# A cached-attention decode block with wq loaded by rows of 112, 8 and 8, and w1 loaded and multiplied block by block

## The chip, the cores and the metric

The kernel runs on one core of one Trainium2 chip. The metric is the device time of one execution in microseconds. A profile of one execution goes with it; its span runs from the first to the last instruction of the program.

## The reference

Four rows (batch 4, one token each) of width 640 pass through an attention block with a cache of 4096 keys and values for each of 32 heads of 128, and then through a dense block with the Mish activation. All inputs are bf16.

```python
def _A_ref(x, k_cache, v_cache, wq, wo):
    q = (x @ wq).reshape(B, Sq, H, Dh).transpose(0, 2, 1, 3)
    scores = jnp.einsum("bhqd,bhkd->bhqk", q, k_cache) * (Dh ** -0.5)
    o = jnp.einsum("bhqk,bhkd->bhqd", _softmax(scores), v_cache)
    return o.transpose(0, 2, 1, 3).reshape(B, Sq, H * Dh) @ wo

def _B_ref(x, w1, b1, w2):
    h = jnp.einsum("bsd,df->bsf", x, w1) + b1
    sp = jnp.log1p(jnp.exp(-jnp.abs(h))) + jnp.where(h > 0, h, 0)
    return jnp.einsum("bsf,fd->bsd", h * jnp.tanh(sp), w2)

h = x + _A_ref(_layernorm(x), k_cache, v_cache, wq, wo)
out = h + _B_ref(_layernorm(h), w1, b1, w2)
```

Sizes: wq is 640 x 4096, wo 4096 x 640, w1 640 x 1728, w2 1728 x 640. Keys and values are 134 MB each.

## The kernel before

The program sets its own order: what is written first is issued first on each engine. Everything that is large comes by DMA on SP's queue; only x and b1 come by ACT's queue.

Three slots of 64 KB per partition hold all large data in turn. The first holds wq (with x and b1 behind it). wq is read with five consecutive rows on each of the 128 partitions, so one partition's share is 40,960 contiguous bytes. Then keys and values alternate: `load_kv` brings the keys (`kt`) or the values (`vt`) of eight heads of one batch row, 8 MB, and there are 16 such units u. A load is issued when its slot comes free. The values of the last unit come in four transfers (`VQ`), the others in one.

- `qT_ps` (L200): q for all heads, 160 products; `q_broadcast` spreads one unit's q over the partitions.
- `scores(u)`: DVE multiplies the keys by q in place (L261), PE sums over d with an identity (L268), DVE reduces (L249).
- `softmax(u)`: maximum, broadcast, and eight exponentials on ACT (L307).
- `pv(u-1)`: 64 products with the values (L323). `close(u)` normalizes the result (L338 to L352).

After the last unit's scores the slot `wend` takes wo in four transfers (L386) and w1 in two (L389). `w1_sb` has five row blocks of 128 rows each; `W1P = 4` of them come in the first transfer, the fifth in the second. The slot `wend2` takes w2: its last 64 rows (L395), and the rest in three transfers for chunks 0 to 7, 8 to 11 and 12 (L397).

Then, once per execution and everything in transposed form (width on the partitions):

- `regroup` and `project` (L419 to L436), four times, one for each part of wo: the attention output times wo into `yT`.
- L459: `hT` = x + yT. `column_means` (L463, L467) gives the mean; L474 writes `h2T` = hT minus the mean, the input of the dense block, not yet divided by the deviation.
- h1 (L489): F = 1728 is cut into 13 chunks of 128 and one of 64, fourteen in all. Each chunk is a sum over the five row blocks of w1, so there are 70 products into `h1_ps`. `h1_pass(c, dcs)` does chunk c for the row blocks `dcs`: first all fourteen chunks with the first four blocks, then all fourteen with the fifth. After the fifth chunk of the first round stands the variance (L467), whose square root and reciprocal give `rstd`.
- L514 to L540: scaling, bias and Mish on DVE and ACT.
- y2T (L549): 70 products with w2, the 64-row chunk first, then chunks 0 to 12. Then the sum with hT, a transpose (L561) and the store (L570).

Of the kernel before, what the change touches and what calls it, by code (L numbers as in the profile page):

```python
# [16 lines left out]
def kernel(  # L17
# [13 lines left out]
    nc = tc.nc  # L31
# [5 lines left out]
    DC = D // 128  # L37
# [19 lines left out]
    C2 = F // 128  # L57
    FM = C2 * 128
    FREM = F - FM
    FC = C2 + 1  # L60
    W2P = (0, 8, 12, C2)
    W1P = 4

    ctx.enter_context(tc.manual_schedule())

# [13 lines left out]
    def slot(name):  # L79
        return slots.tile([128, SLOT], BF16, tag="kv", name=name)  # L80
# [13 lines left out]
    wq_sb = first[:, 0 : DC * H * Dh].rearrange("p (c n) -> p c n", c=DC)  # L94
# [3 lines left out]
    b1_row = first[0:1, o0 + 2 * D : o0 + 2 * D + F]  # L98

    nc.scalar.dma_start(out=x_bf, in_=x_rows[:, :])  # L100
    nc.sync.dma_start(out=wq_sb, in_=A_wq.rearrange("(p c) n -> p c n", c=DC))
    nc.scalar.dma_start(out=b1_row, in_=B_b1.rearrange("(o f) -> o f", o=1))
    kts, vts = {}, {}
    kts[0] = load_kv("kt", A_k_cache, 0)
# [53 lines left out]
    for src, dst in ((ln1_v, xT), (x_v, xT_res)):  # L158
# [10 lines left out]
        out=own1[:, :], in_=ident[:, :].rearrange("p (i k) -> p i k", i=G), axis=AX.X, op=ALU.add  # L169
    )  # L170
    nc.vector.tensor_scalar(
        out=own[:, :], in0=own1[:, :], scalar1=-1.0, scalar2=1e30, op0=ALU.add, op1=ALU.mult
    )
    nc.vector.tensor_reduce(
        out=sel[:, :, :],
        in_=ident[:, :].rearrange("p (t i r) -> p r i t", t=CT, r=RQ),
# [5 lines left out]
        out=dq_f[:, :], in_=ident[:, :].rearrange("p (q j) -> p q j", j=J), axis=AX.X, op=ALU.add  # L182
# [4 lines left out]
        out=j_f[:, :], in_=ident[:, :].rearrange("p (q j) -> p j q", j=J), axis=AX.X, op=ALU.add  # L187
# [3 lines left out]
    def f_chunk(rows, c):  # L191
        if c < C2:
            return rows[:, 0:FM].rearrange("p (f k) -> p k f", k=C2)[:, c, :], 128
        return rows[:, FM:F], FREM
# [3 lines left out]
    for h in range(H):  # L198
        for c in range(DC):
            nc.tensor.matmul(  # L200
                qT_ps[:, h, :],
                lhsT=wq_sb[:, c, h * Dh : (h + 1) * Dh],
                rhs=xT[:, c, :],
                start=(c == 0),
                stop=(c == DC - 1),
# [3 lines left out]
    for c in range(FC):  # L209
        cols, fw = f_chunk(b1_row, c)  # L210
# [171 lines left out]
    w1_sb = wend[:, nwo : nwo + DC * F].rearrange("p (c f) -> p c f", c=DC)  # L382
# [2 lines left out]
    for o in range(NO):  # L385
        nc.sync.dma_start(out=wo_sb[:, o], in_=wo_view[:, o])  # L386
    w1_view = B_w1.rearrange("(c p) n -> p c n", p=128)
    for c0, c1 in ((0, W1P), (W1P, DC)):
        nc.sync.dma_start(out=w1_sb[:, c0:c1], in_=w1_view[:, c0:c1])  # L389
    wend2 = slot("wend2")  # L390
    nw2 = FC * D
    w2_sb = wend2[:, 0 : C2 * D].rearrange("p (k n) -> p k n", k=C2)
# [8 lines left out]
    def scratch(n, dt=FP32):  # L401
        a = at[0]
        w = n * (2 if dt == FP32 else 1)
        w += w % 2
        at[0] = a + w
        ap = wend2[:, a : a + w]
        return ap.bitcast(FP32)[:, 0:n] if dt == FP32 else ap[:, 0:n]
# [53 lines left out]
    def column_means(src, name):  # L461
        part = scratch(N)
        nc.vector.tensor_reduce(  # L463
            out=part, in_=src.rearrange("p c n -> p n c"), axis=AX.X, op=ALU.add
        )
        m_ps = ps.tile([128, N], FP32, tag="oT", name=f"{name}_ps")
        nc.tensor.matmul(m_ps[:, :], lhsT=mean_f, rhs=part, start=True, stop=True)  # L467
        return m_ps
# [4 lines left out]
    for dst in (h2T, hc):  # L473
        nc.vector.tensor_tensor(  # L474
            out=dst,
# [7 lines left out]
    h1_ps = ps.tile([128, FC, N], FP32, tag="qq", name="h1_ps")  # L483
    nc.vector.memset(h1_ps[FREM:128, FC - 1, :], 0.0)
    rstd = scratch(N)
    def h1_pass(c, dcs):
        fw = f_chunk(w1_sb[:, 0, :], c)[1]
        for dc in dcs:
            nc.tensor.matmul(  # L489
                h1_ps[0:fw, c, :],  # L490
                lhsT=f_chunk(w1_sb[:, dc, :], c)[0],
                rhs=h2T[:, dc, :],
                start=(c == 0 and dc == 0),
                stop=(c == C2 - 1 and dc == DC - 1),
            )

    for c in range(FC):
        h1_pass(c, range(W1P))
        if c == 4:
            v_ps = column_means(sq, "var")  # L500
            std = scratch(N)
            nc.scalar.activation(
                out=std, in_=v_ps[:, :], func=ACT.Sqrt, bias=eps_t[:, :], scale=1.0
            )
            nc.scalar.activation(out=dummy[:, :], in_=eps_t[0:N, :], func=ACT.Exp)
            nc.vector.reciprocal(out=rstd, in_=std)
    for c in (C2, *range(C2)):
        h1_pass(c, range(W1P, DC))

    def fcn():  # L510
        return scratch(FC * N).rearrange("p (c n) -> p c n", c=FC)
# [3 lines left out]
        out=h1n,  # L515
# [6 lines left out]
        out=h1s,  # L522
# [8 lines left out]
        out=tb, in0=ta, scalar=2.0, in1=ta, op0=ALU.add, op1=ALU.mult  # L531
# [3 lines left out]
        out=tc_, in0=tb, scalar1=-0.5, scalar2=-1.0, op0=ALU.mult, op1=ALU.add  # L535
# [5 lines left out]
        out=act_t, in0=td, scalar=1.0, in1=h1s, op0=ALU.add, op1=ALU.mult  # L541
# [4 lines left out]
    for i, (w2, c) in enumerate(w2_of):  # L546
        rows = 128 if c < C2 else FREM
        for dc in range(DC):
            nc.tensor.matmul(  # L549
                y2T[:, dc, :],  # L550
                lhsT=w2[:, dc * 128 : (dc + 1) * 128],
                rhs=act_t[0:rows, c, :],
                start=(i == 0 and dc == 0),
                stop=(i == FC - 1 and dc == DC - 1),
# [3 lines left out]
        out=oT.rearrange("p n c -> p c n"), in0=hT, in1=y2T[:, :, :], op=ALU.add  # L558
# [4 lines left out]
        lhsT=oT.rearrange("p n c -> p (n c)"),  # L563
        rhs=ident[:, :],
        start=True,
        stop=True,
# [35 lines left out]
```

## Time and profile before

| what | value |
|---|---|
| time, median of 3 runs | 671.0 us (670.92 to 671.01) |
| the profiled execution's own time | 670.93 us |
| its span | 669.1 us |
| moved by DMA | 283.78 MB, mean 424 GB/s |
| busy: PE, DVE, ACT | 385.3, 353.3, 86.8 us |
| granted TensorE clock, 100 to 580 us | 0.84 |
| granted TensorE clock from 640 us on | 0.50 |

The span has two stretches. Until about 650 us units of keys and values stream in, and the engines work on each when it has landed. From there on only the projection and the dense block are left. In the timeline each row has its start, its length, the engine, the line, the tiles, the number of instructions and, in brackets, how long the engine had been idle and what ended that. A q after an engine's name is its instruction queue. In the page's list of DMA issues the last number is the time from issue to landing.

### The profile page before, as it was taken

The page shows a single profiled execution, that of the slowest core. Times are in us where ns is not written, and L with a number is a line of the kernel's source. Part 1 is how long each engine was busy: PE and PEld are TensorE (multiplying, and loading weights), DVE is VectorE, ACT ScalarE, POOL GpSimd, SP SyncE. Part 2 cuts the span into 40 slices and gives each one's busy share as a digit, 9 for nine tenths or more (in the row PEclk, how much of TensorE's full clock was granted, in tenths as well). Part 3 has the DMA queues.
Part 4 walks back from the last instruction along what each step waited for, and adds up shares of the span by engine and source line. Part 5 has one row for each costly group of instructions (what it writes and reads, how often), then busy time and mean ns, then how long its engine had stood idle before and what let it go on. Part 6 is the DMA issues. An engine that isn't in the chain of part 4 may idle for free.

```text
span 669.1 us, 6430 instructions
## 1 busy us (share of the span) xinstructions
PE 385.3 (58%) x2793; PEld 182.5 (27%) x2793; DVE 353.3 (53%) x314; ACT 86.8 (13%) x314; POOL 1.4 (0%) x10
## 2 busy tenths in 40 slices
PE   0366758385572738467282855737285673728755
PEld 0322323132231313223031322313132331313345
DVE  2078848183664818275381926648192654818321
ACT  0102020202020020202002020110202020020211
POOL 0000000000000000000000000000000000000000
PEclk9998979689696968979698886969788696978955
DMA  9999999999999999999999999999999999999995
GB/s 377 440 439 432 439 432 435 432 439 424 427 432 439 440 431 416 431 440 439 428 431 428 435 432 439 435 428 435 436 431 432 427 424 435 436 428 415 427 413 187
DMA packets 7013, 283.78 MB, mean 424 GB/s; under 512 B 771, under 2 KB 967, under 8 KB 1736
## 3 DMA queue, kind: packets, MB, share of 16 engines
q1 hardware_dynamic: 6974, 283.35, 98.4%
q8 instruction: 22, 0.36, 0.2%
q14 instruction: 7, 0.06, 0.0%
q10 hardware_dynamic: 10, 0.01, 0.0%
HBM read 283.35 MB, written 0.01 MB: 423 GB/s over the span
## 4 chain that ended last, share of the span: by engine, by line
DMA 59%; DVE 25%; PE 12%; issue 2%; SPq 0%; DVEq 0%; ACT 0%
DMA kt<-in_A_k_cache_dram 55%; DVE kt L261 21%; PE s L268 6%; DMA wend<-in_B_w_dram 5%; PE o L323 4%; DVE s_sb L249 3%; PE h_ps L489 1%; DVE pm L287 1%; PE tr L289 0%; PE tr L300 0%; DVE mx L293 0%; PE y2T L549 0%; SPq L386 0%; DVE otn L352 0%; DVE rl L351 0%
## 5 line engine op out<-in xcount | busy, mean ns | idle before, releaser
L268 PE MATMUL s<-kt,ident 128*128 128x512 bf16 x1024 | 269.5, 417 | 223.4 <-DVE kt L261 223.4
L261 DVE TENSOR_TENSOR kt<-kt,qb 128x4096 bf16<-128x4096 bf16 x128 | 288.2, 2284 | 190.6 <-DMA kt<-in_A_k_cache_dram 190.6
L268 PEld LDWEIGHTS <-ident 128*128 128x128 bf16 x1024 | 108.7, 106 | 377.8 <-issue 148.2
L307 ACT ACTIVATE e<-s_sb,nb 128x256 bf16<-128x256 f32 x128 | 63.1, 494 | 218.7 <-DVE nb L302 218.7
L249 DVE TENSOR_REDUCE s_sb<-s 128x64 f32<-128x512 f32 x64 | 44.0, 688 | 54.4 <-PE s L268 32.5
L323 PE MATMUL o<-vt,e 128*32 128x512 bf16 x1024 | 66.2, 415 | 4.3 <-DMA vt<-in_A_v_cache_dram 4.3
L235 ACT CAST qb<-qb_ps 128x128 bf16<-128x128 f32 x16 | 4.3, 266 | 306.4 <-PE qb_ps L227 306.4
L323 PEld LDWEIGHTS <-e 128*32 128x32 bf16 x1024 | 28.1, 104 | 34.3 <-issue 13.7
L307 ACT ACTIVATION_READ_ACCUMULATOR e<-s_sb,nb 128x1 f32 x128 | 23.8, 186 | 0.0
L289 PE MATMUL tr<-ident_f,pm 128*1 128x128 f32 x32 | 6.1, 270 | 21.3 <-DVE pm L287 21.3
L342 PE MATMUL oT<-sel,o_sb 128*128 128x8 f32 x128 | 17.5, 263 | 1.1 <-ACT o_sb L331 1.1
L342 PEld LDWEIGHTS oT<-sel,o_sb 128*128 128x128 f32 x128 | 16.4, 200 | 1.3 <-ACT o_sb L331 1.3
L351 DVE RECIPROCAL rl<-oT 128x8 f32<-128x8 f32 x16 | 3.2, 202 | 16.9 <-PE oT L342 16.9
L331 ACT COPY o_sb<-o 128x512 f32<-128x512 f32 x16 | 9.1, 569 | 14.6 <-PE o L323 14.6
L200 PE MATMUL qT_ps<-xT,first 128*128 128x4 bf16 x160 | 4.4, 166 | 10.9 <-DMA first<-in_A_wq_dram 10.9
L289 PEld LDWEIGHTS tr<-ident_f,pm 128*1 128x1 f32 x32 | 1.8, 80 | 28.7 <-issue 28.7
L300 PE MATMUL tr<-mx,nscale 1*128 1x8 f32 x32 | 6.1, 262 | 5.9 <-DVE mx L293 5.9
L293 DVE TENSOR_REDUCE mx<-tr 1x8 f32<-1x128 f32 x16 | 4.5, 278 | 9.0 <-PE tr L289 9.0
L214 DVE COPY b1T<-b_ps 128x13 f32<-128x13 f32 x1 | 0.2, 173 | 14.7 <-PE b_ps L211 14.7
L300 PEld LDWEIGHTS tr<-mx,nscale 1*128 1x128 f32 x32 | 4.7, 182 | 10.6 <-DVE mx L293 10.6
L200 PEld LDWEIGHTS <-first 128*128 128x128 bf16 x160 | 4.3, 104 | 11.0 <-DMA first<-in_A_wq_dram 11.0
L338 PEld LDWEIGHTS oT<-rs,ones_f 128*128 128x128 f32 x32 | 6.1, 198 | 3.3 <-issue 1.3
(77 smaller groups left out, 77.0 us busy)
## 6 DMA issues: line engine op xcount, KB each, us to landing
vt<-in_A_v_cache_dram SPq DMA_DIRECT2D x4, 2048.0 KB, 44.0
first<-in_A_wq_dram SPq DMA_DIRECT2D x1, 5120.0 KB, 15.6
wend<-in_A_wo_dram SPq DMA_DIRECT2D x4, 1280.0 KB, 21.2
wend<-in_B_w_dram SPq DMA_DIRECT2D x1, 1728.0 KB
wend<-in_B_w_dram SPq DMA_DIRECT2D x1, 1280.0 KB, 21.0
wend<-in_B_w_dram SPq DMA_DIRECT2D x1, 640.0 KB, 20.2
wend<-in_B_w_dram SPq DMA_DIRECT2D x1, 432.0 KB, 28.2
kt<-in_A_k_cache_dram SPq DMA_DIRECT2D x16, 47.9
```

Source lines behind the costliest of these rows:

```text
L200: nc.tensor.matmul(qT_ps[:, h, :], lhsT=wq_sb[:, c, h * Dh : (h + 1) * Dh], rhs=xT[:, c, :], start=(c == 0), stop=(c == DC - 1),)
L249: nc.vector.tensor_reduce(out=s_sbs[u][:, part * RP : (part + 1) * RP], in_=s_ps[:, :, :], axis=AX.X, op=ALU.add,)
L261: nc.vector.tensor_tensor(out=kt[:, :, d0 : d0 + DQ], in0=kt[:, :, d0 : d0 + DQ], in1=qbs[u][:, d0 : d0 + DQ].unsqueeze(1).to_broadcast([1 ...
L268: nc.tensor.matmul(s_ps[:, :, :], lhsT=ident[:, :], rhs=kt[:, :, d : d + W], start=(d == 0), stop=(d == Dh - W),)
L287: nc.vector.tensor_reduce(out=pm[:, :], in_=s_sb[:, :], axis=AX.X, op=ALU.max)
L289: nc.tensor.matmul(tr_ps[0:1, 0:128], lhsT=pm[:, :], rhs=ident_f[:, :], start=True, stop=True)
L300: nc.tensor.matmul(nb_ps, lhsT=nscale[:, :], rhs=mx[:, :], start=True, stop=True)
L307: nc.scalar.activation(out=e2[:, :, i, :], in_=s_sb[:, :].rearrange("p (g r) -> p g r", r=RQ), func=ACT.Exp, bias=nb[:, i : i + 1], scale= ...
L323: nc.tensor.matmul(o_ps[t : t + G * RQ, :], lhsT=e2[:, g, :, :], rhs=vt[:, g * RQ : (g + 1) * RQ, :], start=(g < CT), stop=(g >= NGV - CT),)
L331: nc.scalar.copy(out=o_sb[:, :], in_=o_ps[:, :])
L342: nc.tensor.matmul(oT_ps[:, 0, :], lhsT=o_sb[:, r * Dh : (r + 1) * Dh], rhs=sel[:, r, :], start=(r == 0), stop=(r == RQ - 1),)
L489: nc.tensor.matmul(h1_ps[0:fw, c, :], lhsT=f_chunk(w1_sb[:, dc, :], c)[0], rhs=h2T[:, dc, :], start=(c == 0 and dc == 0), stop=(c == C2 - ...
```

## The change

wq comes by three transfers on SP's queue instead of one: partitions 0 to 111, 112 to 119 and 120 to 127. w1 comes by five transfers of one row block each, instead of one of four blocks and one of one. The h1 products are reordered: five rounds, one for each row block, of fourteen products (chunk 0, the 64-wide chunk, then 1 to 12). The variance stands after the second round, that is after 28 products instead of 20. The number of products stays the same. wo and w2 are loaded as before.

```diff
-    W1P = 4
...
-    nc.sync.dma_start(out=wq_sb, in_=A_wq.rearrange("(p c) n -> p c n", c=DC))
+    wq_view = A_wq.rearrange("(p c) n -> p c n", c=DC)
+    for p0, p1 in ((0, 112), (112, 120), (120, 128)):
+        nc.sync.dma_start(out=wq_sb[p0:p1], in_=wq_view[p0:p1])
...
-    for c0, c1 in ((0, W1P), (W1P, DC)):
-        nc.sync.dma_start(out=w1_sb[:, c0:c1], in_=w1_view[:, c0:c1])
+    for c in range(DC):
+        nc.sync.dma_start(out=w1_sb[:, c], in_=w1_view[:, c])
...
-    def h1_pass(c, dcs):
-        fw = f_chunk(w1_sb[:, 0, :], c)[1]
-        for dc in dcs:
+    for dc in range(DC):
+        for c in (0, C2, *range(1, C2)):
+            lhsT, fw = f_chunk(w1_sb[:, dc, :], c)
             nc.tensor.matmul(
                 h1_ps[0:fw, c, :],
-                lhsT=f_chunk(w1_sb[:, dc, :], c)[0],
+                lhsT=lhsT,
                 rhs=h2T[:, dc, :],
-                start=(c == 0 and dc == 0),
-                stop=(c == C2 - 1 and dc == DC - 1),
-            )
-
-    for c in range(FC):
-        h1_pass(c, range(W1P))
-        if c == 4:
+                start=(dc == 0 and c == 0),
+                stop=(dc == DC - 1 and c == C2 - 1),
+            )
+        if dc == 1:
             v_ps = column_means(sq, "var")
...
-    for c in (C2, *range(C2)):
-        h1_pass(c, range(W1P, DC))
```

## The prediction

> **What bounds the kernel now.** I read the page first: its slices, then its chain, then its DMA parts.
>
> ```profile
> DMA  9999999999999999999999999999999999999995
> ...
> q1 hardware_dynamic: 6974, 283.35, 98.4%
> q8 instruction: 22, 0.36, 0.2%
> ...
> q10 hardware_dynamic: 10, 0.01, 0.0%
> ...
> DMA 59%; DVE 25%; PE 12%; issue 2%; SPq 0%; DVEq 0%; ACT 0%
> ```
>
> The 16 DMA engines are full in 39 of 40 slices, and 283 MB over 669 us leave nothing to gain but what comes before the first byte and after the last. So I went to the end: the chain in order of time, then the timeline of PE and of SP's queue.
>
> ```profile
> 626.13 30.73 DMA wend<-in_B_w_dram
> 656.86 0.05 issue
> 656.90 1.34 PE h_ps L489 x20
> 658.25 0.43 PE var_ps L467 x2
> 658.67 3.16 PE h_ps L489 x50
> ```
> ```profile
> 652.17 1.23 PE L436 MATMUL yT<-wend,wend 128*128 128x4 bf16 x40 [1.62 <-DMA wend<-in_A_wo_dram]
> 653.98 0.56 PE L467 MATMUL mean_ps<-wend 128*128 128x4 f32 x2 [0.58 <-DVE wend L463]
> 656.90 1.34 PE L489 MATMUL h_ps<-wend,wend 128*128 128x4 bf16 x20 [2.36 <-DMA wend<-in_B_w_dram]
> 658.11 0.57 PE L467 MATMUL var_ps<-wend 128*128 128x4 f32 x2
> 658.53 3.29 PE L489 MATMUL h_ps<-wend,wend 128*128 128x4 bf16 x50
> 663.93 2.10 PE L549 MATMUL y2T<-wend 64*128 64x4 bf16 x70 [2.11 <-DVE wend L540]
> ```
> ```profile
> wend<-in_B_w_dram SPq DMA_DIRECT2D x1, 1280.0 KB, 21.0
> wend<-in_B_w_dram SPq DMA_DIRECT2D x1, 640.0 KB, 20.2
> wend<-in_B_w_dram SPq DMA_DIRECT2D x1, 432.0 KB, 28.2
> ```
>
> PE stands idle for 2.36 us until w1's first transfer, four row blocks in one, is complete at 656.86. The other operand, h2T, has been there since about 654.75: the timeline has L474 start at 654.58, two in 0.26 us. The 56 products of the first four blocks and the 14 of the last, 70 in all, then follow without a hole (1.34 + 0.43 + 3.16 = 4.93 us with the variance between), and all 70 stand between the landing and L514.
>
> The trace also has, for each transfer, the time at which each engine completed its share. The first wo part, for instance, has its sixteen completions from 637.85 to 642.81: the slowest engine is 4.96 us behind the fastest, and a landing is the slowest engine's. I followed each engine by chaining packet records (each begins 3 to 4 ns before the one ahead of it ends). All move a 65,536-byte packet in 2.42 us, so none is slower as such. The lag comes from q8: each 16 KB record takes some 1.05 us and stretches the next packet by 0.5, so one fetch costs its engine 1.5 us. The q8 fetches go round eight engines only, always the same ones in the same order. Just before the end (after 248 such packets) the eight fetched engines lag by 3.06, 3.11, 3.13, 3.21, 3.27, 3.38, 4.66 and 4.96 us, the other eight by 0, 0.21, 0.38, 0.42, 0.43, 1.31, 2.17 and 3.23 (the last two take the larger q14 fetches).
>
> **Part one, w1 and h1.** Removed: the wait for four blocks at once. Added: three more transfers, and an order in which block dc is multiplied into all fourteen chunks before the next. Products stay 70, the variance's two products move from after 20 to after 28.
>
> When do the blocks land? On the fastest engine wo's last part completes at 647.13, the four-block transfer at 651.49, the single block at 652.58: 4.36 us for four, 1.09 for one. By that, blocks follow at 1.09 to 1.26 us (the slowest engine's step from 656.86 to 658.12). From wo's last landing at 652.12: 653.3, 654.5, 655.7, 656.9 and 658.1.
>
> PE starts at 654.85, when h2T is there. A pass takes 14 x 66 ns (3.29 us / 50) = 0.92 us. Passes start at 654.85, 655.77, then after the variance's 0.43 at 657.1, 658.0 and 658.9. The blocks are there 1.5, 1.2, 1.4, 1.1 and 0.8 us earlier: PE becomes the bound, no block is waited for. The last product ends at 654.85 + 70 x 0.066 + 0.43 = 659.9 instead of 661.83: 1.9 us; taking the measured 4.93 us for the whole, 659.8, 2.05 us. I take 2.0.
>
> The variance: its product at about 656.7 instead of 658.11; ACT's Sqrt, the 1.28 us table load and the dummy Exp behind it end 2.4 us after its start (658.11 to 660.49 now), so at 659.1, before L528's Exp at about 660.4. It costs nothing.
>
> Does w2 hold what is gained? L549 starts at 661.9 instead of 663.93. Issue plus the landing times of the third fence: 640.54 + 21.0 = 661.5 for chunks 0 to 7, 642.82 + 20.2 = 663.0 for 8 to 11, 663.48 for chunk 12. At 30 ns a product (2.10 us / 70) chunk 8 is wanted at 661.9 + 45 x 0.03 = 663.25, chunk 12 at 663.85. Cover of 0.25 and 0.4 us: this is the next bound.
>
> SP's queue. The wait view for SP says
>
> ```profile
> SPq L397 <- DMA wend<-in_A_wo_dram: 4.3, 2, 2.7
> SPq L389 <- DMA vt<-in_A_v_cache_dram: 3.3, 1, 3.3
> ```
>
> so an issue waits for the landing of an older transfer. The semaphores repeat every eight transfers: w1's second transfer was released at 629.90 by the second quarter of vt15, eight issues earlier, w2's later two by wo's first and second parts (642.81, 645.89). With three more transfers in between, w2's three are released by wo's third and fourth parts and w1's first block: about 649.0, 652.1 and 653.3 instead of 640.5, 642.8 and 645.9. The fastest engine finishes w2's 64-row piece, all that is ahead, at 653.02, and the two larger parts after it at 656.45 and 658.09. From issue to first packet took 1.0 us on wq (0.74 to 1.77). So the spare is 3.0, 3.3 and 3.8 us, and this costs nothing; without that spare each microsecond of delay would come off directly behind the 0.25 us cover. The store, the only thing behind them on SP, comes at 666.
>
> **Part two, wq.** 112 rows are 7 per engine, as 128 were 8. How do 8 rows spread? q10, ACT's queue, held the 4-row x and the 1-row b1: ten packets, which are four of 1280 bytes, one of 3456 and five completions. Four rows went to four engines, one row to one, so I take eight engines, the same for both small transfers: 9 rows on eight engines, 7 on the rest, at 1.514 us a row (the length of a 40,960-byte packet). At the start this hides: q is broadcast at 22.9 us, the first kt arrives at 35.9. The engines never run dry, so the shift lasts to the end: plus 1.51 us on some eight, minus 1.51 on the others.
>
> Which eight? b1's one engine carried an x row too, so small transfers start from the same engines. Of x's four I can follow two exactly (1.70 and 2.05 us), and neither is among the fetched eight. I take it that the extra rows go to the eight without q8's fetches. Then these lag by 1.51 to 4.74 us and the fetched by 1.55 to 3.45: the slowest is at 4.74 instead of 4.96, and every landing comes 0.2 us earlier, vt15's last quarter, wo and h2T with it.
>
> The Trainium skill, DMA: Bandwidth & Descriptors, section on why a DMA increments its semaphore by 16, has the rule: the engine count is the largest number up to 16 that divides the slowest dimension, and the lowest-numbered engines are used. By that rule 112 rows take sixteen and 8 rows eight; the four completions of x agree, and nothing here numbers the engines.
>
> **Sum.** 2.0 + 0.2 = 2.2 us; span 669.1 to 666.9. The profiled execution took 670.93 us, 1.8 outside the span; 668.7. The median of the runs is 671.0, 0.07 above it: 668.8. About 0.2%, 1.3 us, is what a measurement of this kernel can tell from no change.
>
> **The rivals.**
> *The relief reaches all slow engines.* If the eight relieved include every engine now over 3 us, the one with 3.23 among them, landings come 1.5 us earlier: 2.05 + 1.5 = 3.5, and w2's last part at 663.48 - 1.5 = 662.0 is still in time: 667.5. Against: nine engines are over 3 us, eight are relieved.
> *The extra rows fall on slow engines.* Then vt15, wo, h2T and w2 all land 1.5 us later, and 2.05 - 1.5 leaves 0.5: 670.5. For: two of x's four engines could not be followed. Against: the two that could.
> *Dependencies are coarse:* the first product waits for all of w1, 658.1 + 4.93 = 663.05, 1.2 us late: 672.2. Against: now it starts at 656.90, before the single block's 658.12.
> *Each transfer costs its own fixed time, in series.* The 5 KB of x took from 0.73 to its last completion at 2.42: 1.7 us. Three more such in w1 move w2's last part to 663.3 + 5.1 = 668.4; with 0.15 of products and the 3.1 us from L549's end to the span's, 671.6, that is 2.5 us longer: 673.5. It decides from 0.9 us per transfer (2.2 + 0.4 of cover, over three). Against: the single block followed at 1.09 us.
> The Trainium skill, DMA: Bandwidth & Descriptors, section "Anatomy of one DMA", speaks for that rival: about 2 us fixed plus bytes over 436 GB/s, some 3.0 us for 432 KB, an estimate by which three transfers add 6 us. The trace disagrees, with 1.09 us.
>
> **How the numbers follow.** Forecast 0.60 (own range 668.2 to 669.6: passes of 0.92 to 0.99 us, landings from 0.4 us earlier to 0.6 later); full relief 0.13; extra rows on slow engines 0.16; coarse dependencies 0.03; fixed cost 0.08. Faster is 0.60 + 0.13 with a little of the third: 0.74. Same is the rest of the third and the fourth: 0.18. Slower is the fixed cost: 0.08. The range runs from full relief, 667.3, to the third with some room, 670.8.
>
> **What would show it.** Right: no DMA wait within h1's 70 products (L486 to L495 of before), which run from about 654.6 to 659.6; y2T's from about 661.7 with no hole; the spread of wo's completions near 4.7 us instead of 4.96, the slowest engine one without q8's fetches. Wrong: a spread over 6 us, holes between passes, or y2T waiting for w2.

## The result and the profile after

The changed kernel takes 687.9 us (median of 5 runs, 687.29 to 689.03) against 671.0 before: a ratio of 1.0257, 95% interval 1.0246 to 1.0268. The forecast was 668.8. The profiled execution's span grew from 669.1 to 686.1 us.

The page after: the DMA slices, then the issues of wq (size, time from issue to landing).

```profile
DMA  9999999999999999999999999999999999999995
GB/s 251 147 429 428 429 428 429 432 440 439 429 432 429 439 429 436 433 428 429 429 439 440 429 432 433 428 429 439 425 428 429 439 440 432 444 428 405 423 415 202
...
first<-in_A_wq_dram SPq DMA_DIRECT2D x1, 4480.0 KB, 22.3
```

The engines are as full as before, but in the first two slices they move 251 and 147 GB/s. Below are three stretches, before first and after second. Each line has the stretch, its length, the busy us (and number) of the instructions of PE, PEld (PE's weight loads), DVE, ACT and POOL, then the granted clock, the share of time in which the DMA engines hold a packet, and GB/s:

```profile
0.00:16.00 16.00, 0.62 (x10) 0.48 (x10) 3.67 (x16) 1.58 (x2) 1.19 (x9) 1.00 0.96 394
16.00:36.00 20.00, 5.95 (x176) 5.59 (x177) 0.23 (x3) 2.58 (x6) 0.00 (x0) 1.00 0.97 420
36.00:100.00 64.00, 42.23 (x210) 17.21 (x211) 47.83 (x33) 9.20 (x36) 0.00 (x0) 0.89 1.01 438
```
```profile
0.00:16.00 16.00, 0.62 (x10) 0.48 (x10) 3.68 (x16) 1.58 (x2) 1.18 (x9) 1.00 0.96 246
16.00:36.00 20.00, 0.56 (x22) 0.59 (x23) 0.00 (x0) 0.00 (x0) 0.00 (x0) 1.00 1.03 184
36.00:100.00 64.00, 37.91 (x286) 18.23 (x283) 40.05 (x28) 7.07 (x24) 0.00 (x0) 0.97 0.99 430
```

The share says that the engines hold a packet all the time; the last column says that the packets are slow. In the first 36 us there are 148 GB/s less for 16 us and 236 GB/s less for 20 us: 7.1 MB, or 16.4 us at 432 GB/s. The packet records show it one by one. A 40,960-byte row of wq took 1.51 us before. Of the 112 rows one takes 2.73 us in the median; the first eight rows after them take 4.8 to 6.3 us, the last eight 6.3 to 6.6. The three transfers complete at 23.07, 29.50 and 35.30 us, where wq was complete at 16.31. The engines end their seventh row of wq at 20.0 us in the mean instead of 13.4, so some 6.6 of the 16.4 us are already lost in the 112 rows. The rest goes with the two small transfers, and not in wq alone: the first kt packets of the eight engines that have no part in the first of them take 8.6 to 10.2 us, where such a packet took 2.42. The wait view after has PE standing for wq (us in total, times, longest):

```profile
PE qT_ps L202 <- DMA first<-in_A_wq_dram: 29.5, 1, 29.5
```

Later landings never make that up: vt15's last quarter lands at 657.64 us instead of 639.72, w2's last part at 681.38 instead of 663.48, both 17.9 us later. Of that the fastest engine lost 16.4 (its first wo part completes at 654.21, before at 637.85), the number above; the rest is the spread of wo's completions, 6.5 us instead of 4.96.

The end of the chain after:

```profile
670.10 1.24 PE yT L438 x40
...
673.22 2.13 PE h_ps L491 x28
675.35 0.43 PE var_ps L469 x2
675.78 3.03 PE h_ps L491 x42
```

No DMA stands between wo's last landing and h1's end any more; that part did what was forecast. But the 70 products with the variance take 5.6 us where they took 4.93, and they start 0.45 us after h2T is there. From vt15's last landing to the end of the span there are 28.5 us instead of 29.4: 17.9 lost, 0.9 gained, 17.0 in the span.

### The profile page after: what moved, and what is told of

It is laid out like the page before. It is cut to its first block, busy times and chain, and to the rows that moved or that the text cites. A ratio compares the mean times of both kernels' runs of the same rounds, so it can differ in the third digit from the quotient of the medians.

```text
span 686.1 us, 6438 instructions
## 1 busy us (share of the span) xinstructions
PE 386.4 (56%) x2793; PEld 183.2 (27%) x2793; DVE 353.3 (51%) x314; ACT 86.9 (13%) x314; POOL 1.4 (0%) x10
## 4 chain that ended last, share of the span: by engine, by line
DMA 57%; DVE 25%; PE 14%; issue 2%; another core or an unknown queue 2%; SPq 0%; DVEq 0%; ACT 0%
DMA kt<-in_A_k_cache_dram 48%; DVE kt L263 20%; PE s L270 6%; DMA first<-in_A_wq_dram 5%; PE o L325 5%; DMA wend<-in_A_wo_dram 4%; DVE s_sb L251 3%; PE h_ps L491 1%; PE qT_ps L202 1%; DVE pm L289 1%; PE tr L291 0%; PE tr L302 0%; DVE mx L295 0%; PE y2T L546 0%
## 5 line engine op out<-in xcount | busy, mean ns | idle before, releaser
L325 PE MATMUL o<-vt,e 128*32 128x512 bf16 x1024 | 67.8, 423 | 4.7 <-DMA vt<-in_A_v_cache_dram 4.7
L344 PEld LDWEIGHTS oT<-sel,o_sb 128*128 128x128 f32 x128 | 16.4, 200 | 1.3 <-ACT o_sb L333 1.3
L353 DVE RECIPROCAL rl<-oT 128x8 f32<-128x8 f32 x16 | 3.2, 202 | 17.4 <-PE oT L344 17.4
L289 DVE TENSOR_REDUCE pm<-s_sb 128x1 f32<-128x256 f32 x16 | 6.7, 420 | 0.5
```

Source lines behind the costliest of these rows:

```text
L289: nc.vector.tensor_reduce(out=pm[:, :], in_=s_sb[:, :], axis=AX.X, op=ALU.max)
L325: nc.tensor.matmul(o_ps[t : t + G * RQ, :], lhsT=e2[:, g, :, :], rhs=vt[:, g * RQ : (g + 1) * RQ, :], start=(g < CT), stop=(g >= NGV - CT),)
L344: nc.tensor.matmul(oT_ps[:, 0, :], lhsT=o_sb[:, r * Dh : (r + 1) * Dh], rhs=sel[:, r, :], start=(r == 0), stop=(r == RQ - 1),)
```

## The experiments

**The parts alone.** w1 in five transfers and h1 in five passes, wq whole:

```diff
-    for p0, p1 in ((0, 112), (112, 120), (120, 128)):
-        nc.sync.dma_start(out=wq_sb[p0:p1], in_=wq_view[p0:p1])
+    nc.sync.dma_start(out=wq_sb, in_=A_wq.rearrange("(p c) n -> p c n", c=DC))
```

> Part one alone: w1 in five transfers and h1 in five passes, wq in one transfer as before. By the profile of the changed kernel, the stretch from the landing of vt15's last quarter to the end of the span is 28.46 us where it was 29.42: 0.96 us shorter, so 670.0 us here if the tail is independent of wq. By the prediction's sum it would be 2.05 us, 669.0; the profile after says why not: h1's first product waits for the DVE's memset of h_ps, 0.45 us, and each pass's 64-wide chunk costs some 0.14 us more, 0.68 us in all. If the five transfers themselves cost something that the late wq hid: 671 or more.

Measured: 670.16 us against 670.92, ratio 0.9989 (0.9979 to 0.9998). This part is a gain of 0.8 us, not 2.0. Its w2 transfers are issued at 648.92, 652.05 and 653.15 us and land at 661.5, 663.0 and 663.4, as before the change: the queue order costs nothing, as forecast.

The other part alone, wq by 112, 8 and 8 rows with w1 and h1 as before:

> Part two alone: wq by 112, 8 and 8 rows, w1 and h1 as before. All theories of the wq loss expect 671.0 + 17.9 = about 689 (every landing after wq is 17.9 us later in the changed kernel); if the two parts act on each other, another number.

Measured: 689.12 us in one run, 18.2 more than before. The whole loss is in wq. As far as one run can tell the parts add up: 18.2 less 0.8 is 17.4, the two together cost 16.9, and the changed kernel's own runs lie 1.7 us apart.

**Three transfers, or 8 rows?** wq in three transfers, each of all partitions:

```diff
-    for p0, p1 in ((0, 112), (112, 120), (120, 128)):
-        nc.sync.dma_start(out=wq_sb[p0:p1], in_=wq_view[p0:p1])
+    for c0, c1 in ((0, 3), (3, 4), (4, 5)):
+        nc.sync.dma_start(out=wq_sb[:, c0:c1], in_=wq_view[:, c0:c1])
```

> wq in three transfers again, but each of all 128 partitions: three, one and one of the five 4096-wide blocks. Theory A (the destination: engines that write into neighbouring partitions share one engine's rate, and all 128 partitions together reach everything) expects wq complete at 16 to 17 us as before, 671 us. Theory B (the source rows lie badly in memory) the same, since each engine reads the same rows as before. Theory C (three transfers instead of one, or small ones, are slow in themselves) expects wq some microseconds late and 675 or more.

Measured: 671.58 us, wq complete at 16.20. Three transfers as such cost about 0.7 us, by one run. Left are the destination, the source, the eight engines and, since the pieces here are of 1 to 3 MB, the small size.

**The source.** The small transfers read rows that are 16 apart:

```diff
-    for p0, p1 in ((0, 112), (112, 120), (120, 128)):
-        nc.sync.dma_start(out=wq_sb[p0:p1], in_=wq_view[p0:p1])
+    nc.sync.dma_start(out=wq_sb[0:112], in_=wq_view[0:112])
+    for i, p0 in enumerate((112, 120)):
+        nc.sync.dma_start(out=wq_sb[p0 : p0 + 8], in_=wq_view[i : i + 113 : 16])
```

> wq by 112, 8 and 8 partitions as in the change, but the two small transfers read rows 0, 16, 32 ... 112 and 1, 17 ... 113 of the source instead of 8 neighbouring ones; so the last 16 partitions hold other rows of wq than the reference's. Theory A (the destination decides): packets of 6.4 us again, 689. Theory B (neighbouring source rows are slow to read): packets of about 1.5 us, the small transfers take 3 us together, wq complete at about 26, 677 to 680.

Measured: 689.03 us, packets of the last eight rows 6.5 to 6.6 us, wq complete at 34.95. It isn't that the source rows are neighbours.

**The destination.** First the same 16 rows as two transfers of every second partition (`wq_sb[112:128:2]` and `wq_sb[113:128:2]`):

> wq by 112 rows as in the change, then partitions 112, 114 ... 126 and 113, 115 ... 127 as two transfers of 8 rows; the rest as before. Theory A (engines whose rows lie in the same group of four neighbouring partitions share one engine's rate): two engines to a group instead of four, so packets of 2 x 1.51 = 3.0 us instead of 6.4, wq complete at about 29 us instead of 34.9 and a time of about 683 instead of 689.1. Theory B (the place of the source rows in memory) and Theory C (any 8-row transfer on eight engines is slow): packets of 6.4 us again, 689.

Measured: 684.51 us; packets of 3.2 to 4.5 us; wq complete at 30.31. Then the 16 rows in one transfer (`(0, 112), (112, 128)`):

> wq by 112 and 16 rows; the 16 rows go to sixteen engines, one row each. Theory A: four rows to each of four groups still, so one round of 4 x 1.51 = 6.1 us instead of two, wq complete at about 29, time about 683. Theory C (eight engines instead of sixteen make the small transfers slow): packets of 1.5 us, wq complete at about 25, 677 to 679. Both with the first 112 rows at 23 us as in the change.

Measured: 682.27 us; packets of 4.0 to 5.3 us. One line from the DMA view of each of the two kernels (KB, us from issue to landing):

```profile
first<-in_A_wq_dram SPq DMA_DIRECT2D x1, 4480.0 KB, 21.5
```
```profile
first<-in_A_wq_dram SPq DMA_DIRECT2D x1, 640.0 KB, 26.7
```

The first is the 112 rows with every second partition behind them (landing at 22.2, 23.1 in the change), the second is the 16 rows, issued at 1.2 and so complete at 27.9. With sixteen engines the rows are still slow, so eight engines are not the cause; with the engines spread two to a group instead of four the packets are shorter by about a third. Both times are near Theory A's 683, but its packets are not met: 3.2 to 4.5 us where it says 3.0, 4.0 to 5.3 where it says 6.1. It has the direction, not the exact price.

Then a split into two halves, 64 and 64 rows, four rows for each of sixteen engines:

```diff
...
+    for p0, p1 in ((0, 64), (64, 128)):
+        nc.sync.dma_start(out=wq_sb[p0:p1], in_=wq_view[p0:p1])
```

> wq by two transfers of 64 rows, four rows per engine, each engine's four in one group of four partitions. Theory A in its plain form (a group of four partitions has one engine's rate): no two engines meet, wq complete at 16 to 17 us, 671. Theory A as the Trainium skill has it (SBUF - State Buffer, DMA port swizzle: partitions p and p + 32 are on the same port): by that rule two engines to each port, packets of 3.0 us, wq complete at about 27 us and 681 to 683. Theory C (the number or size of transfers): 671, since both halves use all sixteen engines.

```profile
first<-in_A_wq_dram SPq DMA_DIRECT2D x2, 2560.0 KB, 27.9
```

Measured: 684.42 us; the sixteen last packets of wq take 3.1 to 3.2 us each, twice 1.51 and a little; the second half lands at 29.3. The time is 1.4 us over the range of Theory A's second form, and far from the 671 of its plain form and of Theory C. The plain form of Theory A falls if, as it takes for granted, each engine has four neighbouring partitions of its own: they still run at half speed. No run shows which rows an engine has. The Trainium skill, SBUF — State Buffer, section on the DMA port swizzle, says that partitions p and p + 32 are on the same one of sixteen ports; by that rule 64 neighbouring partitions have eight ports, and the packets here, twice as long, agree.

**The disputed cost by itself.** wq whole, then two small transfers that nothing reads:

```diff
...
+    for k, (p1, st) in enumerate(((8, 1), (32, 4))):
+        nc.sync.dma_start(
+            out=first[0:p1:st, o1 + 4608 * k : o1 + 4608 * (k + 1)], in_=wq_flat[0:8, 0:4608]
+        )
```

> wq in one transfer as before, then two added transfers of 8 rows by 9216 bytes each into a free part of the first slot, not read by anything: the same 8 rows of wq, first into partitions 0 to 7, then into partitions 0, 4, 8 ... 28. Theory A: in the first, four engines share each group of four partitions, 4 x 0.34 us (9216 bytes at 40,960 bytes per 1.514 us), about 1.4 us per packet; in the second each engine has a group of its own, 0.34 us. Theories B and C (the source, or small transfers on eight engines): both alike, and if the slowdown seen in the changed kernel (6.4 us for 1.5) were that, 1.4 us each. The Trainium skill, SBUF - State Buffer, section on the DMA port swizzle, has four neighbouring partitions on one port, which is Theory A.

Measured: 671.44 us, which decides nothing: the first packet of each engine took 0.35 to 0.73 us, the second 0.41 to 1.05, so the neighbours' writes were still draining when the spread ones came. Neither form of the expectation was met. So each kind got a run of its own, `((8, 1), (8, 1))` and `((32, 4), (32, 4))`:

> As the probe, but both added transfers of 8 rows by 9216 bytes go into partitions 0 to 7 (different columns). Theory A: 16 packets of 9216 bytes share the rate of two engines (2 x 40,960 bytes per 1.514 us, 54 GB/s), so 2.7 us from the first packet's start to the last one's end, and the second packet of each engine near 1.4 us or more. Theory C (eight engines are slow): the same in this run.

> As the probe, but both added transfers go into partitions 0, 4, 8 ... 28, from the same source rows on the same eight engines. Theory A: no two engines meet, all 16 packets take 0.34 us and each engine is through both in 0.7 us. Theory C: as slow as the run with neighbouring partitions.

Measured: with partitions 0 to 7 the packets take 0.35 to 1.39 us, and all sixteen 2.8 us from the first start to the last end (14.63 to 17.44), against 2.7 by two engines' rate. The second packet of each engine, 0.72 to 1.39 us, stays under the 1.4 expected. With partitions 0, 4 ... 28 all sixteen take 0.347 us. Same eight engines, same source rows, same bytes: the number of engines, the source and the small size are out, and the destination is left. The times, one run each, are 672.88 us near and 670.97 far, against 671.12 without either. From the chains (start, length), near first, kt0 lands at 37.55 and at 35.96 us:

```profile
1.92 35.63 DMA kt<-in_A_k_cache_dram
```
```profile
2.70 33.26 DMA kt<-in_A_k_cache_dram
```

In the stretches of the two kernels, near first:

```profile
16.00:18.00 2.00, 0.24 (x9) 0.24 (x10) 0.00 (x0) 0.00 (x0) 0.00 (x0) 1.00 0.62 201
```
```profile
16.00:18.00 2.00, 1.59 (x59) 1.59 (x60) 0.00 (x0) 0.00 (x0) 0.00 (x0) 1.00 1.13 492
```

201 against 492 GB/s in 2 us. A packet counts where it starts, so one stretch exaggerates; from 14 to 20 us it is 370 against 457 GB/s, while the small transfers hold only 147 KB. The engines that have no part in them are slowed too: the first kt packets take 4.07 us beside the near transfers and 2.42 beside the far ones. So a crowded destination stops more than its own writers. What couples them was not tried, and no run takes the 112 rows apart: that their 2.73 us come from the destination too is inferred.

**The tail.** The memset of h_ps moved ahead of hT's sum:

```diff
+    h1_ps = ps.tile([128, FC, N], FP32, tag="qq", name="h1_ps")
+    nc.vector.memset(h1_ps[FREM:128, FC - 1, :], 0.0)
     hT = scratch(DC * N).rearrange("p (c n) -> p c n", c=DC)
...
-    h1_ps = ps.tile([128, FC, N], FP32, tag="qq", name="h1_ps")
-    nc.vector.memset(h1_ps[FREM:128, FC - 1, :], 0.0)
```

> w1 in five transfers and h1 in five passes, wq in one transfer, and the memset of h_ps moved on DVE ahead of hT's sum, into its idle time before the last wo product. If h1's first product waited for that memset (it began 0.45 us after h2T's was written), h1 starts 0.4 us earlier: 669.7 against 670.16 without the move. If it waited for something else, 670.2.

Measured: 669.66 us against 670.90, ratio 0.9982 (0.9973 to 0.9991). Then also the five 64-wide products in one run:

```diff
     for dc in range(DC):
-        for c in (0, C2, *range(1, C2)):
+        if dc == DC - 1:
+            for d in range(DC):
+                h1_product(d, C2)
+        for c in range(C2):
...
+            h1_product(dc, c)
```

> As the run with the memset moved, and the five products of the 64-wide chunk in one run ahead of the last pass instead of one in each pass. If the switch between 128-wide and 64-wide weights costs 0.14 to 0.17 us per visit, five visits become one: 0.6 to 0.7 us off, 669.1. If w1's blocks, or w2, then come late, less: w2's last parts land at 663.0 and 663.4 and its products for chunk 8 would be wanted at about 663, so a gain over 2.2 us against before is not expected.

Measured: 668.97 us against 670.90, ratio 0.9971 (0.9959 to 0.9982). Two lines of DVE with w1 alone, then PE's timeline with w1 alone, then with both steps:

```profile
654.97 0.06 DVE L483 MEMSET h_ps<- 64x4 f32 x1
655.00 0.19 DVE L462 TENSOR_REDUCE wend<-wend 128x4 f32<-128x20 f32 x1
```
```profile
655.18 2.18 PE L488 MATMUL h_ps<-wend,wend 128*128 128x4 bf16 x28 [0.73 <-DVE wend L462]
657.64 3.16 PE L488 MATMUL h_ps<-wend,wend 128*128 128x4 bf16 x42
662.91 2.10 PE L543 MATMUL y2T<-wend 64*128 64x4 bf16 x70 [2.11 <-DVE wend L534]
```
```profile
654.75 1.67 PE L487 MATMUL h_ps<-wend,wend 128*128 128x4 bf16 x26 [0.27 <-DVE wend L475]
656.71 2.92 PE L487 MATMUL h_ps<-wend,wend 128*128 128x4 bf16 x44
661.74 2.10 PE L549 MATMUL y2T<-wend 64*128 64x4 bf16 x70 [2.11 <-DVE wend L540]
```

The bracket shows the first step: the idle time before h1 falls from 0.73 to 0.27 us, and it now ends with L475, which writes h2T, instead of L462, the instruction after the memset. L462's result is no operand of h1; that moving the memset alone takes the wait away shows that it hung on the memset. Why PE starts 0.15 us after the memset's end isn't shown. The second step is in the lengths: from the first product to the end of the last 5.62 us (655.18 to 660.80) became 4.88 (654.75 to 659.63). This is the fastest version run here, faster than both kernels.

## Why the prediction was wrong

**The price of a wq row** is the term that failed, in size and in sign: "at 1.514 us a row (the length of a 40,960-byte packet)". That row comes from a transfer into all 128 partitions. It was carried over to transfers into eight neighbouring partitions, where the changed kernel measures 4.8 to 6.6 us, and into 112, where it measures 2.73. For wq the sum had 0.2 us gained; every landing after it came 17.9 us later, and wq alone costs 18.2. I took "none is slower as such" for "a packet has one price"; wq_src, wq_64 and the two last probes show that the price depends on where the packets of the other engines land. The form of 8 rows into 8 neighbouring partitions at once is not in the trace of before; x, four rows of 1280 bytes with packets of 0.05 to 0.09 us, is too small to show it. Such an operation should have been bounded from both sides; it was given one price. Its upper bound, all eight rows at one engine's rate, would have been 8 x 1.51 = 12 us per small transfer, and the measured 4.8 to 6.6 lie within it. For the 112 rows no such bound was drawn either. The Trainium skill, SBUF — State Buffer, says in the part on two DMAs for both halves that only one transfer that spans all 128 partitions reaches all sixteen ports. By that rule the change loses, the runs agree, and the prediction did not weigh it.

**The cover of wq's load** could not save it. "At the start this hides: q is broadcast at 22.9 us, the first kt arrives at 35.9" looks for who waits for wq, and there the cover was 13 us. The sentence behind it has the other half right: the engines never run dry, so what they lose lasts to the end. With one price for a row that shift was 1.51 us up on some and down on the others; with the measured ones it is 16.4 us on the fastest engine, kt0 lands at 54.3 us instead of 35.9, and the cover is beside the point.

**Which engines get the extra rows.** Assumed were the eight without q8's fetches. In the packet records after, five of the eight fetched engines carry seven rows of wq and at least two carry nine. The two engines of x that could be followed did not stand for the rest: the two groups are mixed, and the spread of wo's completions grew to 6.5 us where 4.7 was forecast. The engines also come out of the small transfers unevenly; these runs don't separate the two. The prediction calls q14's fetches the larger ones; their records have 8192 bytes, q8's 16,384.

**None of the rivals** held the cause. *Each transfer costs its own fixed time* was the one on the right side, for another reason: w1_only refutes it for w1, where w2 lands as before, and wq_cols for wq. The section of the Trainium skill that the prediction sets beside it, "Anatomy of one DMA", gives its 2 us for transfers issued from GpSimd; those here are issued by SP and ACT. The price was not in the transfers' number but in their shape.

**w1 and h1.** Right: no block is waited for, PE becomes the bound, w2's releases by wo's third and fourth parts and w1's first block, w2 in time. Too large: 2.0 us forecast, 0.8 measured (0.9 in the changed kernel's spans). The two missing terms are each shown by a run. h1's first product waits for the memset (L484 of before) that stands behind L474 and L481 on DVE; before, the wait for w1 hid it: 0.45 us. And the products were priced at 66 ns each in any order; in the trace of before the step between two of them is 0.06 us, but 0.13 where the width of the weights changes from 128 to 64 and again where it changes back, with 0.08 after it. Before, that happened once, now in each pass: 5.6 us instead of 4.93. With both removed the gain is 1.9 us, near the 2.0 of the sum.

## What to carry to other kernels

A transfer's price belongs to its shape: price a packet from a row whose destination covers the same partitions, and keep transfers on all 128 of them, cutting along the free dimension where pieces are wanted. Where the DMA engines are full from end to end, nothing that slows them is hidden, whoever waits or doesn't. When a DMA wait is taken away, look at once for the next wait of the same instruction (here a memset queued on another engine) and for what a new order of products does to the weights' shape.

## What the runs showed of the hardware

- Eight engines writing 8 neighbouring partitions move what two engines move: 147 KB in 2.8 us, where eight spread partitions take each packet at full rate, 0.347 us for 9216 bytes. Two transfers of 64 neighbouring partitions run at half rate: 3.2 us a row of wq instead of 1.51.
- Engines outside a crowded transfer slow down with it: kt packets of 4.07 instead of 2.42 us beside 2.8 us of small writes.
- A change of the weights' width between 128 and 64 costs PE 0.05 to 0.09 us each way beyond the usual 0.06 us step, at a granted clock of 0.50 (steps of 0.108 to 0.147 us in w1_only).
